# One level of a seven-product scheme in the value matmuls, with the weight sums streamed from DRAM

## The chip, the cores and the metric

The kernel runs on one core of a Trainium2 chip. Its engines work side by side: TensorE (PE; matmuls, with PEld for the weight loads), VectorE (DVE), ScalarE (ACT), GpSimd (POOL) and SyncE (SP), whose queue issues the DMAs here. The metric is the device time of one execution in microseconds.

## The reference

Local and global attention over 8 batches and 8 heads, and then a feed-forward on the attention's output, with a shift by one token:

```python
s_g = scale * q_g @ k_all^T;  out_g = softmax(s_g) @ v_all        # 32 global queries, all 544 keys
s_l = scale * [q_l @ k_g^T, q_l @ k_l^T within 32 positions]      # 512 local queries
out_l = softmax(s_l) @ [v_g, v_l]
x = concat([out_g, out_l])                      # (8, 544, 512): batch, tokens, heads x 64
x_prev = x shifted by one token, zero first
xk = mu_k * x + (1 - mu_k) * x_prev;  xr likewise with mu_r
k = relu(xk @ w_k)                              # 512 -> 1024
v = (k * k) @ w_v                               # 1024 -> 512
return sigmoid(xr @ w_r) * v
```

The weights w_k, w_v, w_r arrive as 64-bit floats.

## The kernel before

Everything is kept with features on the 128 partitions and tokens along the free side, 256 tokens (TOK) to a feed-forward step. A batch has two such halves of 256 local tokens; the 8 x 32 global tokens of all batches make one more set, done last. Heads are done in pairs of units, a unit being two heads.

A matmul operand of full precision is split into a high part (rounded to the PE's fp32r type by ACT) and a low part (the rest, a subtraction on POOL or DVE), and each product is made of three matmuls, high x high, high x low and low x high (`products`, L383 to L385). One such matmul has 128x128 weights and 256 columns. For one set of 256 tokens the keys take 8 x 4 x 3 = 96 of them, the gates 4 x 4 x 3 = 48, the values 4 x 8 x 3 = 96.

Weights come as chunks of 128x512 64-bit words (512 KB) into three buffers of the pool `stage`. `decode` (L171 to L182) makes 32-bit values of a chunk with one operation on ACT, three on DVE, and splits it with one on ACT and one on POOL. The high and low parts of all three weight matrices then stay in SBUF.

A pair of units runs through `scores` (matmuls L241, masked minimum on DVE L246, exponentials on ACT L251, normalizing on POOL L260), transposes on PE (L273, L282, L322) with copies out of PSUM, and `weighted` (L339, L352, L364). `weighted` begins with two banks of the PSUM tag "t", one of which the second reduction of `scores_global` (L303) reads until it is done. The result goes to `xT`. The feed-forward of a set is `mix` (L408 on DVE, L412 on DVE, L416 on ACT, L417 on POOL), `keys_and_gate` (keys: relu L429 on ACT, square L431 on POOL, high part L434 on ACT, low part L435 on DVE; gates: L446, or L449 and L451), and `values`, whose result is multiplied with the gate on DVE (L463) and stored by SP (L474, L479). All products of the feed-forward use two banks of PSUM, tag "m".

The order: the first batch's heads are done in halves while the weights of the keys arrive. Then `beside_heads` interleaves two generators in proportion to their numbers of steps: the heads of batch b, 32 steps, and the feed-forward of the batch before. The first such stage takes the heads of the second batch with the rest of the first batch's feed-forward (`rest_of_first`, 18 steps: two of keys, two of gates, six of keys and gates, eight of values, with a chunk or two decoded in each of the first ten). Later stages have 20 steps of 24 matmuls (the first of them 16): `feed_forward` makes the values of the set before while the mix of the next one is prepared. The last batch's feed-forward and the global tokens run alone. Within this program order a planner places each instruction by its own estimate of when its inputs are ready, and so also fixes the order in each engine's queue.

## Time and profile before

| | |
|---|---|
| median of 3 runs | 714.57 us (713.87 to 714.68) |
| the profiled execution | 713.56 us, span 711.8 us |
| PE, DVE, ACT, POOL busy | 684.2, 360.0, 394.8, 298.6 us |
| mean granted clock of PE | 0.978 |
| moved by DMA | 66.73 MB, mean 94 GB/s |

The profile shows one execution. "Busy" is the time that an engine has an instruction under way; matmuls overlap each other, so the spacing of their starts tells what one costs. L383 is line 383 of the kernel. "PE ps_t L339 <- DVE mg L303" in the waits says that PE's instruction of line 339, writing ps_t, waited for DVE's of line 303.

### The profile page before, as it was taken

Reading aid. Unit: us, or ns where it says so; the run is one execution under the profiler, and the core shown is the slowest. Engines: PE = TensorE matmul, PEld = TensorE weight load, DVE = VectorE, ACT = ScalarE, POOL = GpSimd, SP = SyncE. Lnnn points to the kernel's source line nnn. Section 1 sums busy time; section 2 is a strip of 40 time slices with the busy share of each in tenths; the row PEclk is TensorE's granted clock in tenths of the full one; section 3 lists DMA queues with packets and bytes.
Section 4 is the critical chain, followed back from the end, with each engine's and each line's share of the span. In section 5 each row is a group of like instructions: output and inputs, shape, how many; then the busy total and the mean of one; then the engine's idle time right before and its main releaser. Section 6 shows DMA issues by size and latency. Waiting matters only on the chain.

```text
span 711.8 us, 18514 instructions
## 1 busy us (share of the span) xinstructions
PE 684.2 (96%) x7616; PEld 645.3 (91%) x7616; DVE 360.0 (51%) x1134; ACT 394.8 (55%) x1075; POOL 298.6 (42%) x325
## 2 busy tenths in 40 slices
PE   5789799999999999999999999999999999999997
PEld 3568689989999999999999999899999999999997
DVE  5797976347254362736354363636354352534511
ACT  5877976365565565646565565646565553332420
POOL 6577685136253353424243353424243351323420
PEclk9788889999999999999999999999999999999999
DMA  8735334151423040403222040403222020000000
GB/s 343 279 98 205 128 124 167 39 179 38 158 74 107 16 164 31 164 32 96 98 84 97 17 163 31 164 30 107 88 90 91 16 80 26 17 16 30 2 30 30
DMA packets 21716, 66.73 MB, mean 94 GB/s; under 512 B 2176, under 2 KB 10880, under 8 KB 21632
## 3 DMA queue, kind: packets, MB, share of 16 engines
q1 hardware_dynamic: 21632, 65.55, 25.9%
q8 instruction: 60, 0.98, 0.6%
q14 instruction: 24, 0.20, 0.1%
HBM read 56.63 MB, written 8.91 MB: 92 GB/s over the span
## 4 chain that ended last, share of the span: by engine, by line
PE 77%; DVE 9%; ACT 7%; issue 3%; POOL 2%; DMA 2%; SPq 0%; POOLq 0%; DVEq 0%
PE ps_m L383 21%; PE ps_m L385 20%; PE ps_m L384 20%; PE ps_t L273 4%; PE ps_t L339 4%; PE ps_s L241 3%; ACT Pt L251 3%; DVE xfull L412 2%; PE ps_t L364 2%; DVE Pt L246 2%; POOL k L431 1%; DVE kkl L435 1%; DMA raw_qk<-qk 1%; PE ps_t L322 1%; PE ps_s L352 1%
## 5 line engine op out<-in xcount | busy, mean ns | idle before, releaser
L383 PE MATMUL ps_m<-xkh,wk_h 128*128 128x256 f32 x544 | 157.0, 290 | 2.5 <-ACT gate L446 2.5
L383 PE MATMUL ps_m<-kkh,wv_h 128*128 128x256 f32 x544 | 154.7, 284 | 0.0
L384 PE MATMUL ps_m<-xkl,wk_h 128*128 128x256 f32 x544 | 153.6, 283 | 0.0
L385 PE MATMUL ps_m<-xkh,wk_l 128*128 128x256 f32 x544 | 152.9, 281 | 0.0
L385 PE MATMUL ps_m<-kkh,wv_l 128*128 128x256 f32 x544 | 151.2, 278 | 0.3 <-POOL wv_l L182 0.3
L384 PE MATMUL ps_m<-kkl,wv_h 128*128 128x256 f32 x544 | 151.0, 278 | 0.0
L260 POOL TENSOR_TENSOR Pt<-Pt,ssum 128x512 f32<-128x512 f32 x64 | 67.8, 1060 | 156.0 <-DVE ssum L211 152.6
L251 ACT ACTIVATE Pt<-Pt,m 128x160 f32<-128x160 f32 x256 | 106.5, 417 | 40.6 <-DVE m L246 39.6
L431 POOL TENSOR_TENSOR k<-relu 128x512 f32<-128x512 f32 x68 | 73.4, 1079 | 125.8 <-ACT relu L429 125.8
L429 ACT ACTIVATE relu<-ps_m 128x512 f32<-128x512 f32 x68 | 40.6, 596 | 125.0 <-PE ps_m L385 122.8
L383 PEld LDWEIGHTS ps_m<-xkh,wk_h 128*128 128x128 f32 x544 | 104.0, 192 | 4.5 <-ACT gate L446 2.8
L383 PEld LDWEIGHTS ps_m<-kkh,wv_h 128*128 128x128 f32 x544 | 102.2, 188 | 3.6 <-issue 2.8
L384 PEld LDWEIGHTS ps_m<-xkl,wk_h 128*128 128x128 f32 x544 | 104.9, 193 | 0.0
L385 PEld LDWEIGHTS ps_m<-xkh,wk_l 128*128 128x128 f32 x544 | 104.0, 191 | 0.0
L385 PEld LDWEIGHTS ps_m<-kkh,wv_l 128*128 128x128 f32 x544 | 102.2, 188 | 0.5 <-POOL wv_l L182 0.5
L384 PEld LDWEIGHTS ps_m<-kkl,wv_h 128*128 128x128 f32 x544 | 102.2, 188 | 0.0
L435 DVE TENSOR_TENSOR kkl<-k,kkh 128x512 fp32r<-128x512 f32 x68 | 51.4, 756 | 98.0 <-POOL k L431 96.9
L246 DVE CUSTOM_DVE_ANT_0 Pt<-ps_s,masks 128x160 f32<-128x160 f32 x256 | 66.9, 318 | 45.7 <-PE ps_s L241 45.7
L383 PE MATMUL ps_m<-xrh,wr_h 128*128 128x256 f32 x272 | 79.6, 293 | 0.0
L384 PE MATMUL ps_m<-xrl,wr_h 128*128 128x256 f32 x272 | 76.9, 283 | 0.0
L385 PE MATMUL ps_m<-xrh,wr_l 128*128 128x256 f32 x272 | 76.8, 282 | 0.0
L417 POOL TENSOR_TENSOR xkl<-xfull,xkh 128x512 fp32r<-128x512 f32 x34 | 44.7, 1314 | 74.3 <-ACT xkh L416 74.3
(93 smaller groups left out, 1279.6 us busy)
## 6 DMA issues: line engine op xcount, KB each, us to landing
raw_qk<-qk SPq DMA_DIRECT2D x32, 768.0 KB, 5.7
raw_v<-v SPq DMA_DIRECT2D x32, 640.0 KB, 4.9
out_l<-gate SPq DMA_DIRECT2D x32, 256.0 KB, 2.2
w<-w_k SPq DMA_DIRECT2D x8, 512.0 KB, 9.3
w<-w_v SPq DMA_DIRECT2D x8, 512.0 KB, 3.6
w<-w_r SPq DMA_DIRECT2D x4, 512.0 KB, 3.9
out_g<-gate SPq DMA_DIRECT2D x2, 256.0 KB, 2.1
mu_k_sb<-mu_k SPq DMA_DIRECT2D x1, 2.0 KB, 11.2
```

What stands on the lines that cost most here:

```text
L246: nc.vector.tensor_tensor_reduce(out=Pt[:, i], in0=place(e, t, h), in1=masks[:, e, slots[t][1]], op0=ALU.add, op1=ALU.min, scale=-scale, s ...
L251: nc.scalar.activation(Pt[:, i], Pt[:, i], AF.Exp, bias=low_x[:, i:i + 1], scale=-1.0, accum_out=ssum[:, i:i + 1],)
L260: nc.gpsimd.tensor_mul(out, Pt[:, each, at:at + n], rinv.unsqueeze(2).to_broadcast([P, 4, n]))
L273: nc.tensor.transpose(tp[:, i], r.Pt[:, 4 * e + i, SG * e:SG * e + W], ident)
L339: nc.tensor.matmul(op[t][h * D:(h + 1) * D, j, e, a], s.v[:, h, i], r.PT[:, e, 2 * t + h, a * BL:(a + 1) * BL], start=(t, h) not in begun, ...
L383: nc.tensor.matmul(out, w_h[:, i, cols], x_h(i), start=(i == 0), stop=False)
L384: nc.tensor.matmul(out, w_h[:, i, cols], x_l(i), start=False, stop=False)
L385: nc.tensor.matmul(out, w_l[:, i, cols], x_h(i), start=False, stop=(i == n - 1))
L417: nc.gpsimd.tensor_sub(lo[:, both], xf, hi[:, both].bitcast(F32))
L429: nc.scalar.activation(rk, kp, AF.Relu)
L431: nc.gpsimd.tensor_mul(k2, rk, rk)
L435: nc.vector.tensor_sub(kl, k2, kh.bitcast(F32))
```

## The change

The values of a batch, 1024 -> 512 features for two halves of 256 tokens, are taken as a 2 x 2 product of blocks. The left side is the weights: A11, A12, A21, A22, each 256 output features by 512 input features. The right side is the squared keys: B11, B21 of the first half of tokens, B12, B22 of the second. Eight block products become seven, with four sums of weights S1 to S4 and four of keys T1 to T4 (Winograd's form of Strassen's scheme); a block product is 24 matmuls (`Keys.product`).

- The sums of weights are made once (`value_weights`, two chunks at a time). The high and low parts of all eight left blocks are written to a DRAM tile `scratch`, and w_v no longer stays in SBUF. Before each product its left block, 1 MB, is read back by two DMAs of SP (`load_left`) into five buffers of half a block each; the first two blocks are requested up front, and each product requests one more behind it. The global tokens' values stay four block products.
- The squared keys are kept unsplit (`k2p`, one buffer per block). The sums T1 to T4 are made by DVE on 128x1024 (`differences`), T1, T3 and T4 in the place of B11, B12 and B21. A block is split when it is near its use, by ACT and DVE (B) or by ACT and POOL (T).
- Products are joined in two banks "m" by going on accumulating in a bank, by copies to `sump` on ACT, and by additions on DVE. Two of a batch's four products with the gate are on POOL.
- Per batch `values_1` (three products) follows the first half's mix of the next batch, `values_2` (four products) that of the second half. So the first batch's values stand beside the third batch's heads instead of the second's: `rest_of_first` has ten steps, all of keys and gates, and the later stages 19. `mix` of the first batch's second half is called once for the keys and once for the gates.
- From the third batch on, each group of matmuls in `scores` and `weighted` is issued as one unbroken sequence (`Run`), whose first matmul waits for the copies and reductions that the group depends on.

```diff
-    gatep = ctx.enter_context(tc.tile_pool(name="gatep", bufs=2))
+    gatep = ctx.enter_context(tc.tile_pool(name="gatep", bufs=3))
     tmpp = ctx.enter_context(tc.tile_pool(name="tmpp", bufs=3))
-    mlp1 = ctx.enter_context(tc.tile_pool(name="mlp1", bufs=1))
-    mlp = ctx.enter_context(tc.tile_pool(name="mlp", bufs=2))
+    sump = ctx.enter_context(tc.tile_pool(name="sump", bufs=3))
+    k2p = ctx.enter_context(tc.tile_pool(name="k2p", bufs=1))
+    dramp = ctx.enter_context(tc.tile_pool(name="dramp", bufs=1, space=bass.MemoryType.DRAM))
     ps4 = ctx.enter_context(tc.tile_pool(name="ps4", bufs=4, space=PSUM))
...
+        order = list(range(src.shape[0] // P))
+        if src is w_v:
+            order = [i + a for i in range(NF // 2) for a in (0, NF // 2)]
...
+    LEFT = ("A11", "A21", "A12", "A22", "S1", "S2", "S3", "S4")
+    HC = NF // 2
...
+    def value_weights():
+        for i in range(HC):
+            A, S = (sums.tile([P, 4, 2, TOK], F32R, tag="x", name=f"left_{x}") for x in "as")
+            s = sums1.tile([P, 4, TOK], F32, tag="s", name="s")
+            a = []
+            for j in range(2):
+                val = decode(staged.pop(0), "s").rearrange("p (j n) -> p j n", j=2)
+                split(val, A[:, 2 * j:2 * j + 2, 0], A[:, 2 * j:2 * j + 2, 1])
+                a.append(val)
+            nc.vector.tensor_add(s[:, 0], a[0][:, 1], a[1][:, 1])
+            nc.vector.tensor_sub(s[:, 2], a[0][:, 0], a[0][:, 1])
+            nc.vector.tensor_sub(s[:, 1], s[:, 0], a[0][:, 0])
+            nc.vector.tensor_sub(s[:, 3], a[1][:, 0], s[:, 1])
+            split(s, S[:, :, 0], S[:, :, 1])
+            for j, part in ((0, A), (4, S)):
+                nc.sync.dma_start(out=scratch[:, j:j + 4, i], in_=part.bitcast(F32))
+            load_chunk()
+            load_chunk()
+            yield
+    V1 = (("A11", "B11"), ("A12", "B21"), ("S2", "T2"))
+    V2 = (("S3", "T3"), ("S1", "T1"), ("A22", "T4"), ("S4", "B22"))
+    to_load = [a for a, _ in V1 + V2] * B + ["A11", "A21", "A12", "A22"]
+    left = []
+    def load_left():
+        if to_load:
+            a = LEFT.index(to_load.pop(0))
+            for i in range(0, HC, 2):
+                part = leftp.tile([P, 2, 2, TOK], F32R, tag="a", name="a")
+                nc.sync.dma_start(out=part.bitcast(F32), in_=scratch[:, a, i:i + 2])
+                left.append(part)
...
+        run = Run(reads["s"] if slots[0][0].b > 1 else None)
...
+    class Run:
+        def __init__(self, copies=None):
+            self.copies, self.last = copies, None
+        def matmul(self, *a, **kw):
+            if self.copies is None:
+                nc.tensor.matmul(*a, **kw)
+                return
+            if self.last is not None:
+                with tc.issue_after(self.last.ins), tc.high_priority():
+                    self.last = nc.tensor.matmul(*a, **kw)
+                return
+            self.last = nc.tensor.matmul(*a, **kw)
+            for c in self.copies:
+                tc.add_manual_dep(
+                    self.last.ins, c.ins.name,
+                    mybir.DependencyInfo(mybir.DependencyClass.Sync, mybir.DependencyReason.DATA),
+                )
+    reads = {"s": []}
...
+    def weighted(units, xTs, PG=None, pairs=range(2), bank="s", copies=None):
...
-                nc.scalar.activation(kh, rk, AF.Square)
-                nc.vector.tensor_sub(kl, k2, kh.bitcast(F32))
...
+        def gates(self, whole_gate=True):
             self.gate = gatep.tile([P, NC, TOK], F32, tag="gate", name="gate")
...
                     nc.scalar.activation(self.gate, self.gate, AF.Sigmoid)
...
-            for e0 in range(0, NC, 2):
-                vp = psum("m").rearrange("p (j n) -> p j n", j=2)
+        def write(self, half, v):
+            es = slice(2 * half, 2 * half + 2)
+            o = self.gate[:, es]
...
+    class Keys:
+        def __init__(self, tokens):
+            self.tokens = tokens
+            self.k, self.parts = {}, {}
+        def block(self, name):
+            self.k[name] = k2p.tile([P, HC, TOK], F32, tag=name, name=name)
+            return self.k[name]
+        def keys(self, t):
+            n = self.tokens.index(t) + 1
+            return t.keys([self.block(f"B{i}{n}") for i in (1, 2)])
+        def differences(self):
+            k = self.k
+            k["T1"], k["T3"], k["T4"] = k["B11"], k["B12"], k["B21"]
+            for out, a, b in (("T1", "B12", "B11"), ("T2", "B22", "T1"), ("T3", "B22", "B12"), ("T4", "B21", "T2")):
+                nc.vector.tensor_sub(k[out] if out != "T2" else self.block("T2"), k[a], k[b])
+        def split(self, *names):
+            for b in names:
+                self.parts[b] = []
+                for i in range(0, HC, 2):
+                    h, l = (rightp.tile([P, 2, TOK], F32R, tag=x, name=f"b{x}") for x in "hl")
+                    split(self.k[b][:, i:i + 2], h, l, nc.vector if b[0] == "B" else nc.gpsimd)
+                    self.parts[b].append((h, l))
...
+        def product(self, out, b, fresh=True):
+            right = self.parts.pop(b)
+            for i in range(HC):
+                a, (b_h, b_l) = left[i // 2], right[i // 2]
                 for j in range(2):
...
+                    a_h, a_l = (a[:, i % 2, x, j * P:(j + 1) * P] for x in range(2))
+                    for n, (w, x) in enumerate(((a_h, b_h), (a_h, b_l), (a_l, b_h))):
+                        nc.tensor.matmul(
+                            out[:, j], w, x[:, i % 2], start=fresh and (i, j, n) == (0, 0, 0),
+                            stop=(i, n) == (HC - 1, 2), skip_group_check=True,
+                        )
+            del left[:HC // 2]
+            load_left()
...
+        def values_1(self):
+            t = self.tokens[0]
+            X, Y = self.bank(), self.bank()
+            self.product(X, "B11")
+            c11, self.u2 = self.sum(), self.sum()
+            nc.scalar.copy(c11, X)
+            yield
+            self.product(Y, "B21")
+            nc.vector.tensor_add(c11, Y, c11)
+            t.write(0, c11)
+            yield
+            self.product(X, "T2", fresh=False)
+            nc.scalar.copy(self.u2, X)
+            yield
+            self.split("T3", "T1", "T4")
+        def values_2(self):
+            t0, t1 = self.tokens
+            u2, u3 = self.u2, self.sum()
+            X, Y = self.bank(), self.bank()
+            self.product(X, "T3")
+            nc.vector.tensor_add(X, X, u2)
+            nc.scalar.copy(u3, X)
+            self.split("B22")
+            yield
+            self.product(Y, "T1")
+            nc.vector.tensor_add(u3, Y, u3)
+            t1.write(1, u3)
+            yield
+            self.product(X, "T4", fresh=False)
+            t0.write(1, X)
+            yield
+            self.product(Y, "B22", fresh=False)
+            nc.vector.tensor_add(u2, Y, u2)
+            t1.write(0, u2)
+            yield
+        def values_of_one(self):
+            t, = self.tokens
+            banks = self.bank(), self.bank()
+            for b in range(2):
+                parts = self.parts[f"B{b + 1}1"]
+                for e, out in enumerate(banks):
+                    self.parts[f"B{b + 1}1"] = parts
+                    self.product(out, f"B{b + 1}1", fresh=not b)
+                    if b:
+                        t.write(e, out)
+                    yield
...
+    FF_STEPS = 6
+    V_STEPS = len(V1) + len(V2)
...
-    def feed_forward(tokens, before):
-        for t in tokens:
+    def feed_forward(this, before):
+        for n, t in enumerate(this.tokens):
             t.mix()
-            if before is not None:
-                yield from before.values()
-            yield from t.keys_and_gate()
-            before = t
+            yield from (before.values_1, before.values_2)[n]()
+            if n:
+                this.split("B11", "B21")
+            yield from this.keys(t)
+            if n:
+                this.differences()
+                this.split("T2")
+            yield from t.gates()
     PAIR_STEPS = 8
...
+                weighted(pair, xTs, PG, copies=A.copies + C.copies + [copy, reads["g"]] if pair[0].b > 1 else None)
             for s in nxt or ():
...
-            yield
-        for t in first:
-            yield from t.values()
+        yield from first[0].gates(whole_gate=False)
+        first[1].mix("r")
+        yield from first[1].gates(whole_gate=False)
...
+        leftp, rightp = place(ctx, "leftp", 5, side="right"), place(ctx, "rightp", 6, side="right")
+        load_left()
+        load_left()
+        last.split("B11", "B21")
+        last.differences()
+        last.split("T2")
+    leftp = rightp = None
     beside_heads(rest_of_first(), 2 * FF_STEPS - 2)
-    last = None
+    before = last
     for b in range(1, B):
-        tokens = tokens_of(b) + ([global_tokens()] if b == B - 1 else [])
-        steps = feed_forward(tokens, last), FF_STEPS * len(tokens) - (4 if last is None else 0)
+        this = Keys(tokens_of(b))
+        steps = feed_forward(this, before), 2 * FF_STEPS + V_STEPS
         if b < B - 1:
             beside_heads(*steps)
-        last = tokens[-1]
-    for _ in steps[0]:
-        pass
-    for _ in last.values():
+        before = this
+    final = Keys([global_tokens()])
+    t, = final.tokens
...
+        yield from steps[0]
+        t.mix()
+        yield from before.values_1()
+        yield from final.keys(t)
+        yield from t.gates()
+        yield from before.values_2()
+        final.split("B11", "B21")
+        yield from final.values_of_one()
+    for _ in end():
         pass
```

116 lines of the change are left out of this document (58 added, 58 removed).

## The prediction

> **What bounds the kernel now.** I read the head of the page first (busy shares, 40 slices, chain), then the busy time by stretch, then the waits.
>
> ```profile
> span 711.8 us, 18514 instructions
> PE 684.2 (96%) x7616; PEld 645.3 (91%) x7616; DVE 360.0 (51%) x1134; ACT 394.8 (55%) x1075; POOL 298.6 (42%) x325
> ...
> PE   5789799999999999999999999999999999999997
> ...
> ACT  5877976365565565646565565646565553332420
> ...
> PEclk9788889999999999999999999999999999999999
> ```
>
> From the seventh slice on TensorE never rests and the others are half idle; in the first six DVE and ACT are as full as PE, and PE's clock is not always whole. So there are two regimes. The stretches (columns: busy us and count of PE, PEld, DVE, ACT, POOL; granted clock; DMA share; GB/s) put numbers to them:
>
> ```profile
> core 0: us, PE busy (x) PEld busy (x) DVE busy (x) ACT busy (x) POOL busy (x), PEclk, DMA share, GB/s
> 62.00:115.00 53.00, 48.27 (x518) 43.12 (x517) 44.71 (x119) 45.49 (x116) 35.76 (x33) 0.90 0.45 146
> 115.00:149.00 34.00, 33.68 (x407) 31.97 (x408) 14.04 (x57) 14.18 (x50) 12.43 (x15) 1.00 0.29 107
> 208.80:248.70 39.90, 39.51 (x462) 37.77 (x462) 19.07 (x67) 23.25 (x64) 15.52 (x17) 1.00 0.25 87
> 614.46:625.34 10.88, 10.88 (x98) 10.88 (x97) 3.28 (x4) 2.31 (x3) 3.67 (x3) 1.00 0.07 26
> 636.22:641.98 5.76, 5.76 (x50) 5.76 (x49) 4.50 (x8) 1.85 (x3) 2.45 (x2) 1.00 0.00 0
> ```
>
> 62 to 149 us is the stage in which the second batch's heads run beside the first batch's feed-forward. Until 115 us DVE and ACT are 84% and 86% busy, with queues that wait for each other: that is their limit. From 115 us on PE alone is full. The third row is one steady period, a pair of heads and half a feed-forward. The last two rows are runs of 96 value matmuls and of 48 gate matmuls (the counts take in a neighbour at each edge): 10.88/96 = 113.3 ns and 5.76/48 = 120.0 ns apiece.
>
> **The change, part by part.**
>
> *Products.* A batch's values take 2 x 96 = 192 matmuls now and 7 x 24 = 168 after, of the same shape; the global tokens keep 96. Over eight batches 192 fewer: 192 x 113.3 ns = 21.8 us of PE. If the new operands run at the gates' 120.0 ns instead, the 1344 that stay cost 1344 x 6.7 ns = 9.0 us more; I take 0, since shape and order of an (h, l) triple are the same, and keep 9.0 for the range.
>
> *Where the saving lands.* After 149 us the old kernel has 14 x 240 + 240 = 3600 feed-forward matmuls left. The new one, once its first stage is over, has 8 x 168 values, 14 x 144 keys and gates and 240 of the global tokens: 3600 as well. Heads are equal. So the whole gain is what the first stage gets shorter: it loses all of the first batch's 192 value matmuls. PE needs 48.27 + 33.68 - 21.8 = 60.2 us there; the old stage was 87 us, 65.2 without its values. But those values were PE work that filled the time after DVE and ACT had finished. Their new load, from these groups (out<-in, shape, count | busy us, mean ns | idle before, releaser):
>
> ```profile
> L435 DVE TENSOR_TENSOR kkl<-k,kkh 128x512 fp32r<-128x512 f32 x68 | 51.4, 756 | 98.0 <-POOL k L431 96.9 <-PE ps_m L384 1.1
> L434 ACT ACTIVATE kkh<-relu 128x512 fp32r<-128x512 f32 x68 | 43.3, 636 | 1.6
> L463 DVE TENSOR_TENSOR gate<-ps_m,gate 128x512 f32<-128x512 f32 x34 | 23.5, 691 | 94.1 <-PE ps_m L385 94.1
> L408 DVE TENSOR_TENSOR diff<-xT 128x256 f32<-128x256 f32 x64 | 32.3, 543 | 14.8 <-ACT xT L375 14.3
> L412 DVE SCALAR_TENSOR_TENSOR xfull<-diff,mu_r_sb,xT 128x256 f32<-128x256 f32 x64 | 46.6, 763 | 13.8 <-POOL xkl L417 13.8
> L412 DVE SCALAR_TENSOR_TENSOR xfull<-diff,mu_k_sb,xT 128x256 f32<-128x256 f32 x64 | 36.0, 598 | 1.2 <-POOL xkl L417 1.2
> L417 POOL TENSOR_TENSOR xkl<-xfull,xkh 128x512 fp32r<-128x512 f32 x34 | 44.7, 1314 | 74.3 <-ACT xkh L416 74.3
> L416 ACT CAST xkh<-xfull 128x512 fp32r<-128x512 f32 x34 | 20.9, 616 | 29.2 <-DVE xfull L412 29.2
> L181 ACT CAST wv_h<-w 128x512 fp32r<-128x512 f32 x8 | 5.3, 662 | 0.6 <-DVE w L178 0.6
> ...
> 117.34 1.48 POOL L182 TENSOR_TENSOR wv_l<-w,wv_h 128x512 fp32r<-128x512 f32 x1
> ```
>
> DVE, 62 to 149 us: 44.71 + 14.04 = 58.8. Off: 6 kkl (4.5), 4 gate products (2.8), and the second batch's mix, which now stands beside values (4 x 0.543 + 8 x 0.68 = 7.6; 0.68 is the mean of L412's two rows). On: 16 sums and differences of 128x256 in the weight combinations (8.7 at L408's price), 4 differences more since the second half's mix is made in two goes (2.2), 4 differences of 128x1024 of the squared keys (8 x 0.756 = 6.0), 4 splits of B11 and B21 (3.0). Result 63.8. ACT: 59.7 - 6 x 0.636 - 4 x 0.616 of the moved mix + 8 x 0.66 for casting S (its 128x1024 is no cast of this trace; the bounds are one and two casts of 128x512, and I take two) + 6 x 0.616 = 62.4. POOL: 48.2 + 8 x 1.31 (S) + 2 x 1.31 (T2) - 4 x 1.31 = 56.1. All three pass or near PE's 60.2, and DVE at its 84% needs 63.8/0.844 = 75.6 us. The stage ends at 62 + 75.6 = 137.6 instead of 149: **-11.4 us**; 10.4 of the 21.8 are lost as PE idle time. Bounds: -21.8 (PE stays the limit) and 0.
>
> The route of the left blocks lies inside this stage: weight sums to DRAM (8.4 MB), then two blocks back, only after the early pools close, so after the last split. The last row is the last weight chunk's split, at 117 us; with the sums about 10 us later, and the values are not first needed before 137. Hidden; without that cover it costs the landing shown below.
>
> *Heads' matmuls in one run.* Today a pair's last products start before all banks are free:
>
> ```profile
> 492.33 0.49 PE L352 MATMUL ps_s<-PG,raw_v 128*64 128x32 f32 x10
> 493.22 0.69 PE L339 MATMUL ps_t<-PT,raw_v 128*64 128x64 f32 x16 [0.40 <-DVE mg L303]
> ...
> PE ps_t L339 <- DVE mg L303: 3.9, 10, 0.4
> ```
>
> The new dependencies put this wait ahead of the first matmul, where a feed-forward block can be issued instead. Queued behind that first matmul are only the rest of its run; those who wait for them are ACT's copies to xT, with a mix as cover. **-3.9 us**; bounds -5 and +3.9 (the wait stays and covers the whole run).
>
> *Steady batches.* By twice the third row, per batch: ACT 46.5 - 8 x 0.636 + 14 x 0.616 + 3 PSUM copies (1.8) = 51.8; DVE 38.1 + 5.8 (6.0 for the differences, 4.5 for six splits, 4.1 for six products and sums out of PSUM at L463's price, less 6.0 for kkl and 2.8 for gate products); POOL 31.0 + 8 x 1.31 + 2 gate products (2.2) = 43.7; in a period of 79.8 - 2.7 = 77.1 us. No new bound. New waits: three products (T2, T4, B22) go on in a bank that ACT or DVE has just read or written, each with one 24-matmul product (2.7 us) as cover against a copy of 0.6. Bounds: 0, and 24 such places at the 0.40 us that is the one wait left in a steady pair, 9.6. I take **+3**: the old schedule, with alike chains of relu, square and split, shows one surviving wait per pair.
>
> *End without heads.* Blocks are fetched as two loads of 512 KB, 2.5 blocks ahead:
>
> ```profile
> q1 hardware_dynamic: 21632, 65.55, 25.9%
> ...
> raw_qk<-qk SPq DMA_DIRECT2D x32, 768.0 KB, 5.7
> ...
> w<-w_v SPq DMA_DIRECT2D x8, 512.0 KB, 3.6
> ```
>
> The last eight products stand back to back: 2.72 us each for 1.05 MB. The queue moved 65.55 MB in 25.9% of 711.8 us, 355 GB/s while busy, or 2.95 us a block; eight times 0.23 us are covered by the lead. At the rate of two raw_qk loads together (1.57 MB in 5.7 us, 3.8 us a block) 5.5 blocks fall 6 us behind, and the lead takes back 3.2. I take **+1.5**, bounds 0 and 6.
>
> **Sum**, against the profiled execution's 713.6 us (span 711.8): 713.6 - 11.4 - 3.9 + 3 + 1.5 = 702.8. Its time lies 1.0 us under the median shown, 714.6; on the median's scale 703.8, and I say 703.5. A measurement of this kernel tells about 0.2%, 1.4 us, from no change.
>
> **The rivals.**
>
> *The start stays as long as it was.* PE, with less to do, idles and loses its clock; that happens already:
>
> ```profile
> 80.00:85.00 5.00, 2.53 (x24) 1.82 (x24) 4.79 (x15) 4.94 (x10) 5.00 (x7) 1.00 0.00 0
> 85.00:90.00 5.00, 2.79 (x17) 2.07 (x14) 4.94 (x15) 4.97 (x16) 3.79 (x3) 0.51 0.53 153
> 90.00:95.00 5.00, 5.00 (x25) 5.00 (x24) 3.24 (x7) 3.93 (x13) 4.33 (x5) 0.50 0.16 60
> ...
> 55.30 0.41 PE L383 MATMUL ps_m<-xkh,wk_h 128*128 128x256 f32 x1
> 55.52 0.41 PE L384 MATMUL ps_m<-xkl,wk_h 128*128 128x256 f32 x1
> ...
> 83.40 0.39 PE L383 MATMUL ps_m<-xkh,wk_h 128*128 128x256 f32 x1 [2.47 <-ACT gate L446]
> ...
> 89.67 0.69 PE L282 MATMUL ps_t<-ident,Pgl 128*128 128x128 f32 x2 [2.21 <-ACT PT L275]
> ...
> L435 DVE TENSOR_TENSOR kkl<-k,kkh x68: 682/693/1823, 62.2 to 693.3; 128x512 fp32r<-128x512 f32 x68
> ...
> 98.66 1.82 DVE L435 TENSOR_TENSOR kkl<-k,kkh 128x512 fp32r<-128x512 f32 x1
> ...
> 98.61 1.32 POOL L182 TENSOR_TENSOR wv_l<-w,wv_h 128x512 fp32r<-128x512 f32 x1 [1.64 <-ACT wv_h L181]
> ```
>
> At half clock matmuls start 0.21 us apart, not 0.113. If the stage's 240 keys and gates all ran so, PE would need 60.2 + 24 = 84 us, and the stage would end near 147: 713.6 - 2 - 3.9 + 4.5 + 1 = 713. The Trainium skill, "TensorE: Matmul & The Clock Gate", section "Why this matters for your kernels", says the same danger: a gap of some 3 us between bursts halves the clock. By that rule the idle time that I forecast would be paid twice, and this rival's time would be the result; here the two gaps of 2.47 and 2.21 us go with a cold stretch of ten. A second way to the same time is the collision of DVE and POOL: the L435 row gives its shortest, median and longest in ns, and the longest, 1.82 us against 0.69, ran while POOL made a split (last two rows). For it: more two-input work on both engines, in this very stage. Against: from 80 to 85 us PE was half idle and its clock stayed whole.
>
> *PE keeps the whole saving.* If DVE's work overlaps better, the stage is PE's and ends at 127: 704 - 10.4 = 693. For it: POOL and ACT have gaps until 115. Against: DVE's sum.
>
> *Slower: blocks arrive late.* SP's queue is in order, and it stands at stores:
>
> ```profile
> SPq L474 <- DVE gate L463: 210.5, 21, 28.2
> ```
>
> A block's load queued behind a store whose product is still running is issued only at its end, and then the 3.6 us landing meets a 2.7 us product. Four stores a batch, 32 in all, each delaying PE by 3.6 - 2.7 = 0.9 us, give +29; if half of them do, 704 + 15 = 719. It decides from 0.33 us a store on (10.6/32). Against: two blocks are always ahead, and heads lie between most products.
>
> **How the numbers follow.** Forecast 0.68; start as long as before 0.10 (half of it within 0.2%, the rest split); whole saving 0.09; late blocks 0.13. The forecast's own range, from its bounds: 696 to 711. The range of 692 to 714 takes in the whole saving and the long start and leaves out the late blocks and some of the spread at 120 ns: about 0.17. Faster 0.68 + 0.09 + 0.03 = 0.80; same 0.05; slower 0.15.
>
> **What would show it.** Right: PE under 90% busy somewhere from 100 to 137 us while DVE is full; the first values of the batch near 137; steady periods of 77 us a batch; no wait of L339's kind on DVE mg; block loads never among PE's releasers before the last 25 us. Wrong: PE waits for DMA blocks, value matmuls at 120 ns, steady periods of 79 us or more, or a first stage that ends at 127 or after 147.

## The result, and the profile after

The changed kernel takes 749.34 us median (748.53 to 757.44) against 714.22 of the kernel before on the same chip: ratio 1.0517, 95% interval 1.0445 to 1.059. The forecast was 703.5 with a range of 692 to 714; the change makes the kernel slower by 35 us. The profiled execution took 748.53 us. The head of its page, with PE's and the clock's slices:

```profile
span 746.7 us, 18633 instructions
...
PE 682.7 (91%) x7424; PEld 639.9 (86%) x7424; DVE 428.3 (57%) x1178; ACT 428.3 (57%) x1151; POOL 427.6 (57%) x417
...
PE   5889777679998999899999999899989999898997
...
PEclk9779898899999999999999999999999999999899
```

192 matmuls fewer, and PE is as long busy as before (684.2), because some of what is left runs on a halved clock and at a wider spacing. PE is no longer full: 91% instead of 96%, and digits under 9 return in almost every batch.

I cut both spans into stages where ACT writes the last copy of a batch's heads to `xT`: the second batch's stage, the third's, the fourth to seventh, the eighth, and the end without heads. First the kernel before, then the changed one (columns as in the prediction):

```profile
66.40:151.20 84.80, 79.75 (x899) 73.09 (x898) 55.21 (x171) 57.94 (x163) 44.43 (x44) 0.94 0.39 130
151.20:218.00 66.80, 66.41 (x804) 61.86 (x804) 33.99 (x130) 40.99 (x125) 31.18 (x33) 1.00 0.27 97
218.00:537.60 319.60, 316.45 (x3691) 302.54 (x3690) 153.83 (x529) 185.87 (x513) 126.26 (x136) 1.00 0.25 87
537.60:612.80 75.20, 74.81 (x849) 72.75 (x848) 33.10 (x92) 36.34 (x88) 25.43 (x25) 1.00 0.14 49
612.80:711.80 99.00, 95.27 (x832) 95.07 (x830) 33.58 (x55) 25.87 (x39) 26.88 (x23) 1.00 0.07 22
```
```profile
64.90:150.90 86.00, 64.41 (x720) 55.51 (x723) 69.21 (x186) 62.59 (x168) 53.45 (x46) 0.88 0.60 210
150.90:241.40 90.50, 83.80 (x922) 79.46 (x914) 53.43 (x144) 50.31 (x140) 55.21 (x51) 0.96 0.55 196
241.40:561.90 320.50, 308.90 (x3594) 294.71 (x3593) 175.35 (x542) 198.50 (x550) 184.94 (x180) 0.99 0.51 179
561.90:628.70 66.80, 66.80 (x779) 64.84 (x778) 35.85 (x88) 36.18 (x94) 37.24 (x34) 1.00 0.43 157
628.70:746.70 118.00, 107.70 (x879) 106.34 (x878) 49.77 (x70) 35.61 (x59) 54.16 (x43) 0.97 0.47 161
```

Against what fewer matmuls alone would give at 113.3 ns, with the matmuls counted as the rows above count them (PE's x):

| part | before | after | matmuls more or fewer | above that |
|---|---|---|---|---|
| end of the second batch's heads | 151.2 | 150.9 | none counted on: what is saved here (179 in the stage) is idle time | -0.3 |
| third batch's stage | 66.8 | 90.5 | +118 = +13.4 | +10.3 |
| four steady stages | 319.6 | 320.5 | -97 = -11.0 | +11.9 |
| last stage and end | 174.2 | 184.8 | -23 = -2.6 | +13.2 |

By the program's steps the third batch's stage has only 72 matmuls more, and the last part has 24 more; in the trace PE had made some 47 of the later ones by the time the third batch's heads ended, so the table goes by the trace's counts. The last column adds up to 35.1 us; the spans differ by 34.9. So four questions: why the first stage is as long as it was though PE has 15 us less to do in it, and what the third batch's stage, the steady stages and the end lost. The waits of the changed kernel name the steady loss:

```profile
PE ps_m L575 <- DVE gate L527: 17.6, 6, 3.1
PE ps_s L328 <- DMA raw_qk<-qk: 8.2, 5, 5.3
PE ps_m L575 <- ACT sum L593: 5.3, 2, 3.3
PE ps_s L328 <- DVE w L184: 4.8, 2, 3.4
```

Once a batch the first matmul of a value product (L575) waits 3 us for DVE's copy of the gates out of PSUM (L527), which frees the bank; four of the six waits, 11.6 us, lie in the steady stages. DVE's timeline around the first of them, in the third batch's stage, and then PE in the wait and behind it (by stretch):

```profile
222.35 2.12 DVE L558 TENSOR_TENSOR T<-B,B 128x1024 f32<-128x1024 f32 x1
224.39 1.21 DVE L558 TENSOR_TENSOR B<-B,B 128x1024 f32<-128x1024 f32 x1
225.53 2.98 DVE L496 SCALAR_TENSOR_TENSOR xfull<-diff,mu_r_sb,xT 128x256 f32<-128x256 f32 x2
228.43 0.31 DVE L301 CUSTOM_DVE_ANT_0 Pt<-ps_s,masks 128x160 f32<-128x160 f32 x1
...
229.68 1.22 DVE L558 TENSOR_TENSOR B<-B,T 128x1024 f32<-128x1024 f32 x1
...
230.91 0.65 DVE L527 COPY gate<-ps_m 128x512 f32<-128x512 f32 x1
```
```profile
228.00:231.50 3.50, 0.71 (x6) 0.51 (x5) 3.50 (x15) 2.56 (x10) 0.66 (x2) 0.99 0.27 111
231.50:236.00 4.50, 4.38 (x26) 4.25 (x28) 1.43 (x6) 3.84 (x6) 3.70 (x6) 0.63 0.13 12
```

The gates are done at 228.7, but their copy stands behind differences of the squared keys (L558), a mix and the heads' reductions in DVE's queue. Behind the gap PE's clock is 0.63 for 4.5 us; after four of the six such waits (230, 310, 470 and 689 us) it falls, after those at 390 and 550 it does not. The Trainium skill, "TensorE: Matmul & The Clock Gate", section "What's actually happening", has the clock halve after an idle window of about 3.4 us on a free-running window. The trace agrees with a free-running window, since alike gaps cost the clock in some cases and not in others; it doesn't agree with the length, since these gaps were of 2.9 to 3.1 us.

### The profile page after: what moved, and what is told of

Its sections match the earlier page's. It is cut to its first block, busy times and chain, and to the rows that moved or that the text cites. A ratio compares the mean times of both kernels' runs of the same rounds, so it can differ in the third digit from the quotient of the medians.

```text
span 746.7 us, 18633 instructions
## 1 busy us (share of the span) xinstructions
PE 682.7 (91%) x7424; PEld 639.9 (86%) x7424; DVE 428.3 (57%) x1178; ACT 428.3 (57%) x1151; POOL 427.6 (57%) x417
## 3 DMA queue, kind: packets, MB, share of 16 engines
q1 hardware_dynamic: 43136, 136.86, 51.8%
## 4 chain that ended last, share of the span: by engine, by line
PE 68%; DVE 16%; ACT 7%; issue 3%; DMA 2%; POOL 2%; SPq 0%; POOLq 0%; ACTq 0%; DVEq 0%
PE ps_m L575 22%; PE ps_m L464 10%; PE ps_m L465 10%; PE ps_m L466 10%; PE ps_t L332 5%; DVE xfull L496 4%; PE ps_s L332 4%; ACT Pt L307 3%; PE ps_t L353 3%; DVE B L558 2%; DVE Pt L301 2%; DVE T L558 2%; PE ps_s L334 1%; PE ps_t L378 1%; DVE diff L492 1%
## 5 line engine op out<-in xcount | busy, mean ns | idle before, releaser
L575 PE MATMUL ps_m<-bh,a 128*128 128x256 f32 x960 | 192.1, 294 | 24.6 <-DVE gate L527 17.6
L575 PEld LDWEIGHTS ps_m<-bh,a 128*128 128x128 f32 x960 | 158.7, 198 | 28.2 <-DVE gate L527 18.8
L575 PE MATMUL ps_m<-bl,a 128*128 128x256 f32 x480 | 140.0, 292 | 0.0
L316 POOL TENSOR_TENSOR Pt<-Pt,ssum 128x512 f32<-128x512 f32 x64 | 69.8, 1091 | 84.8 <-DVE ssum L265 81.6
L512 POOL TENSOR_TENSOR B<-relu 128x512 f32<-128x512 f32 x68 | 72.6, 1070 | 69.8 <-ACT relu L511 69.8
L575 PEld LDWEIGHTS ps_m<-bl,a 128*128 128x128 f32 x480 | 95.2, 198 | 0.6
L191 POOL TENSOR_TENSOR bl<-B,bh 128x512 fp32r<-128x512 f32 x48 | 63.0, 1335 | 24.5 <-ACT bh L190 24.5
L496 DVE SCALAR_TENSOR_TENSOR xfull<-diff,mu_r_sb,xT 128x256 f32<-128x256 f32 x64 | 61.7, 991 | 15.4 <-POOL B L512 12.6
L190 ACT CAST bh<-B 128x512 fp32r<-128x512 f32 x100 | 60.9, 623 | 16.4 <-PE ps_m L575 15.1
```

Of the source, the lines that this page charges most:

```text
L190: nc.scalar.copy(hi, val)
L191: (engine or nc.gpsimd).tensor_sub(lo, val, hi.bitcast(F32))
L316: nc.gpsimd.tensor_mul(out, Pt[:, each, at:at + n], rinv.unsqueeze(2).to_broadcast([P, 4, n]))
L496: nc.vector.scalar_tensor_tensor(self.shape(xf[:, j]), self.shape(diff[:, j]), mu[:, c0 + j:c0 + j + 1], self.prev(c0 + j), op0=ALU.mult, ...
L512: nc.gpsimd.tensor_mul(k2[f0 // HC][:, f0 % HC:f0 % HC + 2], rk, rk)
L575: nc.tensor.matmul(out[:, j], w, x[:, i % 2], start=fresh and (i, j, n) == (0, 0, 0), stop=(i, n) == (HC - 1, 2), skip_group_check=True,)
```

## The experiments

I worked with these theories. A: in the steady stages DVE's queue makes PE wait. B: the value matmuls are spaced by where their operands lie. C: the vector work of preparing the value weights holds the first two stages. D: what is lost is DVE's stretching of operations while POOL works, so relieving POOL helps. E: the order of the feed-forward around the values matters. Ratios are to the kernel before, with their 95% intervals; 1% is 7.1 us.

**The steady wait (A and D).**

*e1_order*: the differences and T2's split follow the gates in the program.

```diff
             yield from this.keys(t)
-            if n:
-                this.differences()
-                this.split("T2")
             yield from t.gates()
+            if n:
+                this.differences()
+                this.split("T2")
```

> The differences and T2's split stand behind the gates instead of ahead of them; nothing else. Theory A (in each steady batch TensorE waits some 3.1 us for the gate copies of line 527, because DVE makes the 128x1024 differences first; six such waits, 17.6 us): the six waits go, and the time falls by 12 to 18 us, to 731 to 737. Rival (the waits only move: T2 is then late and TensorE waits ahead of the third product): the time stays within 3 us, and T2's split (line 190 or 191) is named as the releaser instead.

1.052 (1.0503 to 1.0537). The wait is the same (17.9 us, 7 times): the planner, which orders by its own estimate of readiness, put DVE's instructions in the same order as before. Program order tests nothing here.

*e2_gact*: the gates' copies out of PSUM (L527) are made by ACT.

```diff
-                nc.vector.tensor_copy(self.gate[:, e0:e0 + 2], rp)
+                nc.scalar.copy(self.gate[:, e0:e0 + 2], rp)
```

> The gates' two copies out of PSUM are made by ACT instead of DVE; the differences stay where they are. Theory A: DVE's queue no longer stands between the gates and the values, the six waits of 3.1 us go, and the time falls by 10 to 18 us (ACT has 0.6 us a copy more). Rival (ACT, with its exponentials, is as late as DVE was): the same waits with ACT named, time within 3 us.

1.0295 (1.0274 to 1.0316): 16 us less. Waits, and the four steady stages:

```profile
PE ps_m L575 <- ACT gate L527: 6.4, 6, 1.1
```
```profile
241.40:551.80 310.40, 305.93 (x3593) 291.89 (x3593) 164.91 (x524) 206.98 (x565) 182.72 (x180) 1.00 0.51 184
```

The wait is a third of what it was, the clock whole, a period 77.6 us instead of 80.1; these four stages give 10.1 of the 16 us. Theory A holds, with a smaller wait left, now for ACT.

*e7_sqact*: ACT makes the keys' squares instead of POOL (L512).

```diff
-                nc.gpsimd.tensor_mul(k2[f0 // HC][:, f0 % HC:f0 % HC + 2], rk, rk)
+                nc.scalar.activation(k2[f0 // HC][:, f0 % HC:f0 % HC + 2], rk, AF.Square)
```

> The changed kernel, with the 68 squares of the keys made by ACT (0.64 us each) instead of POOL (1.07 us each); DVE's instructions are the same ones. Theory D (DVE's operations with two SBUF inputs last up to three times as long while POOL works, and this makes DVE late): DVE's busy time falls from 428 by 8 us or more although it has the same work, TensorE's waits for DVE gate shrink, and the time falls by 8 us or more. Rival (DVE is late because it has more instructions): DVE's time stays, the waits stay, and ACT's 43 us more make the time the same or longer.

1.0553 (1.0534 to 1.0572), no gain. POOL's busy time fell from 427.6 to 363.5 us, DVE's only from 428.3 to 424.4. Theory D falls as a remedy, though the stretching is there: in the changed kernel, shortest, median and longest in ns,

```profile
L558 DVE TENSOR_TENSOR T<-B,B x8: 1196/2120/2297, 151.5 to 682.7; 128x1024 f32<-128x1024 f32 x8
L558 DVE TENSOR_TENSOR B<-B,B x16: 1209/1218/2054, 149.6 to 684.9; 128x1024 f32<-128x1024 f32 x16
L492 DVE TENSOR_TENSOR diff<-xT x68: 407/419/1510, 30.5 to 656.9; 128x256 f32<-128x256 f32 x68
```

and in e7 other operations are the long ones:

```profile
L558 DVE TENSOR_TENSOR T<-B,B x8: 1190/1225/1226, 150.7 to 687.1; 128x1024 f32<-128x1024 f32 x8
L558 DVE TENSOR_TENSOR B<-B,B x16: 1224/2062/2325, 147.5 to 688.2; 128x1024 f32<-128x1024 f32 x16
```

**The spacing (B).** In the compiled programs (no view of the profile shows addresses) the value weights and their moving operands begin at byte addresses with the same remainder modulo 128, 96 and 96, in the changed kernel, and so do the gates', 32 and 32, in both kernels; the operands of the products that ran at 113 ns begin at 96 and 32. *e3_padv* puts 64 bytes between the pools of the two operands of the values; *e11_b_padg* puts as much before the gate weights in the kernel before.

```diff
-        leftp, rightp = place(ctx, "leftp", 5, side="right"), place(ctx, "rightp", 6, side="right")
+        leftp = place(ctx, "leftp", 5, side="right")
+        place(ctx, "shift", side="right").tile([P, 16], F32, tag="shift", name="shift")
+        rightp = place(ctx, "rightp", 6, side="right")
```

```diff
+    shiftp = ctx.enter_context(tc.tile_pool(name="shiftp", bufs=1, reuse_waits="tile"))      # e11
+    shiftp.tile([P, 16], F32, name="shift")
     gatew = ctx.enter_context(tc.tile_pool(name="gatew", bufs=1, reuse_waits="tile"))
```

> The pool of split keys is moved by 64 bytes, so that the values' weights and moving operand no longer have the same address modulo 128. Theory B (matmuls of 128x256 start 120 ns apart where the two addresses agree modulo 128, and 113 where they don't: before, keys and values 96 against 32 and 113 ns, gates 32 against 32 and 120 ns; after, values 96 against 96 and 120 ns): values at 113 ns, 1440 x 6.6 ns = 9 us less, to 740. Rival (the spacing comes from busier engines and DMAs): values stay at 120 ns, time the same.

> The kernel before with the gate weights moved by 64 bytes, nothing else. Theory B: the gates' 816 matmuls at 113 instead of 120 ns, up to 5.4 us less, 707 to 709. Rival (what TensorE saves turns into waits for the heads, as the 1.7 us of the version with sequences suggests): 711 to 712.

e3 gave 1.046 (1.0427 to 1.0494). The same 4 us of value products, in the changed kernel and in e3 (the counts take in two or three matmuls that began before):

```profile
658.50:662.50 4.00, 4.00 (x36) 4.00 (x35) 2.63 (x4) 3.27 (x6) 2.55 (x2) 1.00 0.46 132
```
```profile
658.50:662.50 4.00, 4.00 (x38) 4.00 (x37) 2.63 (x4) 3.27 (x6) 2.56 (x2) 1.00 0.54 154
```

The median distance of starts is 120 ns in the first and 113 in the second; e11's gates went from 120 to 113 too. So B holds for the spacing, as far as two shifts of 64 bytes show it. Its price in time is smaller than the sum says: e3 gained 4 us of 9 (clear of noise against e1, whose engines run in the changed kernel's order, though not against that kernel's own wider interval), with the DVE wait unchanged (17.4 us in 6) and the long runs of keys, whose addresses did not change, at 118 ns instead of 113 (96 in 11.31 us), which nothing here explains. e11 gained nothing, 0.9996 (0.9986 to 1.0007): PE was busy 679.3 us instead of 684.2 and idle that much longer.

**Unbroken groups.** *e5_b_run* gives the kernel before the class `Run`, as in the change, and *e6_b_run_padg* adds e11's 64 bytes. *e12_norun* takes it out of the changed kernel, *e10_run3* lets it begin at the fourth batch.

```diff
-            self.copies, self.last = copies, None      # e12
+            self.copies, self.last = None, None
-        run = Run(reads["s"] if slots[0][0].b > 1 else None)      # e10, likewise in weighted
+        run = Run(reads["s"] if slots[0][0].b > 2 else None)
```

> The kernel before, with the unbroken sequences of scores and weighted (Run) and nothing else of the change. The prediction's step: the wait of line 339 on DVE mg goes (3.9 us in ten places), time 708 to 711. Rival (the wait stays, ahead of the sequence, or the planner's order gets worse): 713 or more.

> The same, and the gate weights moved by 64 bytes, so that they lie 96 modulo 128 against 32 for their moving operand. Theory B: the 816 gate matmuls at 113 instead of 120 ns, 5.4 us less than with Run alone, 703 to 706. Rival (the address plays no part in the gates): as with Run alone.

> The changed kernel without the unbroken sequences. If they gain in the steady batches what they gained in the old kernel (1.7 us in all) and cost 4 us in the start: time 2 to 3 us less, 746. If they hold off TensorE in the new kernel's fuller queues: 5 us less or more. If they are worth the predicted 3.9 us: 753.

> The changed kernel with the unbroken sequences from the fourth batch on instead of the third, nothing else. Theory E: in the start TensorE no longer stands at the first matmul of the third batch's scores (line 334, 4.2 us at 132 us); time 4 to 6 us less, 743 to 745. Rival (DVE and ACT would hold it at the next matmul anyway): within 2 us.

e5: 0.9981 (0.9972 to 0.9991); e6: 0.995 (0.9938 to 0.9963), 709.5 us, short of the 703 to 706 expected but the fastest version that computes the whole reference; e10: 1.0558 (1.0508 to 1.0607); e12: 1.0814 (1.0758 to 1.0869), which every theory missed. In the old kernel the ten waits of 0.4 us went, and five of 0.7 came at PE's next transposes; 1.4 us of the 3.9 were gained. e10 moves nothing: in the changed kernel one batch more or less of it shows no difference. In the changed kernel the same class is worth 21 us (1.0814 against 1.0517). e12's waits and, around one of them, its stretches:

```profile
PE ps_t L328 <- DVE mg L379: 8.8, 5, 1.8
```
```profile
475.00:480.00 5.00, 3.24 (x52) 2.93 (x49) 5.00 (x16) 2.05 (x9) 2.10 (x2) 0.92 0.25 104
480.00:485.00 5.00, 5.00 (x45) 4.44 (x45) 2.73 (x11) 2.32 (x6) 3.60 (x6) 0.50 0.02 3
485.00:490.00 5.00, 5.00 (x26) 4.78 (x25) 1.57 (x3) 1.42 (x4) 1.07 (x2) 0.55 0.68 236
```

It is the same DVE queue: T, B and the mix stand before the reduction mg, PE's group starts and stops in front of it, and then runs ten us at half clock (40 matmuls of heads in 3.9 us, gates 214 ns apart). In the changed kernel the group is held until its inputs are there, and gates are issued in that time. Whether the small matmuls or the gap alone cost the clock was not tried.

**The first two stages (C).** *e4_nos* leaves the sums S1 to S4 out of the changed kernel (not added, split or stored; A blocks are read in their place). *e13_nowv* leaves out the whole preparation of the value weights and stores the raw chunks instead, so that loads, stores and block reads stay.

```diff
-            nc.vector.tensor_add(s[:, 0], a[0][:, 1], a[1][:, 1])      # e4, and the three sums behind it
-            split(s, S[:, :, 0], S[:, :, 1])
-            for j, part in ((0, A), (4, S)):
+            for j, part in ((0, A),):
...
-            a = LEFT.index(to_load.pop(0))
+            a = LEFT.index(to_load.pop(0)) % 4
```
```diff
-                val = decode(staged.pop(0), "s").rearrange("p (j n) -> p j n", j=2)      # e13
...
-            split(s, S[:, :, 0], S[:, :, 1])
-            for j, part in ((0, A), (4, S)):
-                nc.sync.dma_start(out=scratch[:, j:j + 4, i], in_=part.bitcast(F32))
+                w64 = staged.pop(0).bitcast(F32).rearrange("p (j s n) -> p j s n", j=2, s=2)
+                for k in (2 * j, 4 + 2 * j):
+                    nc.sync.dma_start(out=scratch[:, k:k + 2, i], in_=w64)
```

> The sums S1 to S4 of the weights are not made, split or written (the four products that use them read A blocks instead, so this leaves out part of the computation); everything else stays, with the same loads and products. Theory C (the start is held by the vector engines' work for the weights, of which this is 7 us of DVE, 4 of ACT, 10 of POOL and half of the writes): the first values start by 135 instead of 152 us and the time falls by 10 to 20 us. Rival (the start is held by the heads' and keys' own chains, once the first batch's values no longer fill TensorE): it falls by less than 5 us.

> The changed kernel with the value weights not prepared on chip: each loaded chunk goes straight to the scratch tile, so the loads, the 8.4 MB of stores and the reads of left blocks stay, and the decoding, the splits and the sums S1 to S4 (ACT, DVE, POOL) are left out; the left blocks hold raw words. If the engines' queues, filled by this preparation, hold the first two stages (theory C): 152 us instead of 151 for the end of the second batch's heads becomes 128 to 138, the third batch's 241 becomes 205 to 220, and the time falls to 715 to 728 from 749. If the DMAs (stores and reads) or the chain of heads hold them (rival): both ends move by less than 5 us, and the time stays above 740.

e4: 1.0331 (1.0289 to 1.0374), 13 us less. e13: 1.026 (1.0206 to 1.0314), 18 us less. The second batch's heads end at 146.7 and 141.1 us instead of 150.9, the third's at 227.7 and 222.0 instead of 241.4. The first values start at 133 and 130 us instead of 152. e4 came as expected; e13 moved the same way, but by a little less than expected in all three figures. The DMA traffic, which e13 keeps, isn't what holds them. C holds.

*e8_best1* joins e2 and e3, which had helped, with e11's 64 bytes and with three moves that were not tried alone: one sigmoid per half in the first batch (`whole_gate`), a fourth stage buffer and a fourth early chunk.

```diff
-    stage = place(early_s, "stage", 3, side="right")
+    stage = place(early_s, "stage", 4, side="right")
...
-    for _ in range(3):
+    for _ in range(4):
         load_chunk()
...
-        yield from first[0].gates(whole_gate=False)      # likewise first[1]
+        yield from first[0].gates()
```

> The changed kernel with gate copies on ACT, split keys and gate weights moved by 64 bytes, one sigmoid for each half of the first batch too, and four buffers for weight chunks instead of three. By theories A and B: 734 of the gate copies alone, less 9 for the values and 5 for the gates at 113 ns, 720; if buffers and ACT's table loads hold the start, up to 10 less, 710. Rival (the start is held by the amount of vector work and what TensorE saves is lost in waits): 725 to 730, with the first values not before 150 us.

1.0064 (1.0043 to 1.0086), 717.33 us: 31 of the 35 us are back, and the four steady stages take 308.2 us, 77.05 each. What remains is the start. There PE stood still for 5.75 us before a group's first matmul; DVE's and PE's rows:

```profile
120.39 1.51 DVE L220 TENSOR_TENSOR s<-w,w 128x256 f32<-128x256 f32 x1 [0.36 <-POOL left_s L191]
121.82 1.25 DVE L221 TENSOR_TENSOR s<-w 128x256 f32<-128x256 f32 x1
123.00 0.61 DVE L222 TENSOR_TENSOR s<-s,w 128x256 f32<-128x256 f32 x1
123.65 1.37 DVE L223 TENSOR_TENSOR s<-w,s 128x256 f32<-128x256 f32 x1
124.94 0.31 DVE L301 CUSTOM_DVE_ANT_0 Pt<-ps_s,masks 128x160 f32<-128x160 f32 x1
...
127.07 0.50 PE L334 MATMUL ps_s<-raw_qk 64*64 64x160 f32 x1 [5.75 <-issue]
```

The page calls it "issue", but the matmul starts just after the last of eight reductions (126.9), which began only when the four sums were done: 4.7 us of DVE at the stretched rate, where 4 x 0.41 would be 1.6. *e14_best1_nowv* is e8 with e13's edit, *e18_best1_nos* e8 with e4's. *e15_best1_run3* is e8 with e10's edit; *e16_best1_spool* moves the four sums to POOL.

```diff
-            nc.vector.tensor_add(s[:, 0], a[0][:, 1], a[1][:, 1])      # e16, likewise the other three
+            nc.gpsimd.tensor_add(s[:, 0], a[0][:, 1], a[1][:, 1])
```

> The best version of the new scheme so far (717) with the same part left out. Theory C: the third batch's heads end at 195 to 208 instead of 226, and the time is 690 to 700, under the old kernel's 714: seven products would win if their weights came prepared. Rival: more than 708, so even free preparation would bring less than 1 per cent.

> The best version of the new scheme (717) with only the sums S1 to S4 left out (not added, not split, not stored; the A blocks are read in their place), decoding and splits of A kept. Leaving out the whole preparation brought 19 us, and leaving out the sums in the changed kernel 13. If the sums are the larger part: 702 to 707. If decoding and splits, which the old kernel has too, are the larger part: 709 to 715.

> The best version of the new scheme so far (717) with unbroken groups from the fourth batch on instead of the third. In its trace the first matmul of such a group in the start waits 5.7 us (121.3 to 127.1 us), and it starts 0.07 us after the last of DVE's eight reductions. If that wait is what holds the third batch's heads: 711 to 714. If the reductions are late for any kind of issue, because DVE makes the weight sums first (theory C): 716 to 719, the same wait now at another line.

> The best version of the new scheme so far (717) with the four weight sums S1 to S4 of each of four steps made by POOL instead of DVE. If it is DVE's queue alone that holds the heads in the start (the sums take 4.7 us of it in each step): 711 to 714. If the whole chain of preparation counts, whichever engine it stands on, or POOL then stands in the way of its own normalizing and splits: 716 to 725.

e14: 0.981 (0.9794 to 0.9826), 698.61 us; e18: 0.990 (0.9872 to 0.9927); e15: 1.0155 (1.0135 to 1.0176); e16: 1.0092 (1.0075 to 1.0109). e8's first two stages, then e14's:

```profile
66.30:146.40 80.10, 60.49 (x705) 52.68 (x704) 65.28 (x176) 57.95 (x156) 54.61 (x47) 0.89 0.68 241
146.40:226.00 79.60, 78.23 (x895) 74.93 (x894) 46.02 (x135) 50.91 (x142) 49.05 (x47) 0.99 0.54 196
```
```profile
65.90:131.90 66.00, 56.66 (x703) 50.24 (x702) 42.30 (x138) 46.70 (x140) 36.22 (x37) 0.97 0.80 298
131.90:208.10 76.20, 74.83 (x898) 71.35 (x897) 41.52 (x134) 50.25 (x142) 45.74 (x45) 1.00 0.53 193
```

The same matmuls, and without the preparation the first stage is 14 us shorter. Two thirds of the 2.5% are the sums (e18: 1.6%), which only the new kernel has. e15 went past both expectations: unbroken groups at the third batch are worth 6 us in this version. e16 shows that the chain counts, not DVE alone: moved to POOL, the sums let the first stage end 3 us sooner (143.3), but the next takes 7 us longer and ends 4 us later (229.6), with a wait of 4.5 us for a block from DRAM.

*e9_best2*: e8 with `Run` from the fourth batch, the mix behind the first product, and the gates between the last product groups (E).

```diff
-            t.mix()
-            yield from (before.values_1, before.values_2)[n]()
+            values = (before.values_1, before.values_2)[n]()
+            next(values)
+            t.mix()
+            yield
+            yield from values
...
-        yield from t.gates()
         yield from before.values_2()
+        yield from t.gates()
```

> As the version with 717 us, and three more moves: the unbroken sequences only from the fourth batch on, the next mix behind the first block product instead of ahead of it, and in the end the global gates between the last two groups of four products. Theory E (the rest of the loss is waits that a place in a queue makes: 4 to 9 us of the sequences' first matmul in the start, 5 us of ACT's copies behind the mix in the end, 3 us of block loads): 700 to 707, faster than the kernel before. Rival (the vector engines' amount of work in the start sets it): 712 to 716.

1.0121 (1.0107 to 1.0135), worse than e8 and outside both expectations. e15 has the first of the three moves alone and is slower still, so that move is the loss. The other two together gain some 0.3%, with intervals of e9 and e15 that touch, so E is not shown; neither was measured alone.

*e17_b_best_nowv*: e6 with its eight value chunks copied raw to SBUF, the counterpart of e14.

```diff
         hi, lo = high[:, i, cs], low[:, i, cs]
+        if n >= NK + NC:
+            for k, part in enumerate((hi, lo)):
+                nc.sync.dma_start(out=part.bitcast(F32), in_=w64.bitcast(F32)[:, k * CH:(k + 1) * CH])
+            return
```

> The fastest eight-product version (709.5: the old kernel with unbroken groups and the gate weights moved by 64 bytes) with its value weights not prepared either: each of the eight last chunks is copied raw into the high and low parts by DMA, and decoding and splits are left out. It is the counterpart of e14 (698.6), so that the seven products are compared without the preparation on both sides. If the seven products are worth their PE time once the preparation is gone: 702 to 708, above e14. If the old kernel gains as much from it as the new one (18 us): 692 to 699, not above e14, and the scheme has nothing to give.

0.9838 (0.9819 to 0.9857), 702.27 us. It gains 1.1% from it, e8 gained 2.5%. With no preparation on either side the seven products are 0.3% ahead, with intervals that just overlap: not shown to be faster. With decoding and splits on both sides, and the sums neither made nor stored, they are: e18 0.990 (0.9872 to 0.9927) against e6 0.995 (0.9938 to 0.9963). The sums then cost 1.6%.

## Why the prediction was wrong, by its steps

The sum gave 702.8 us for the profiled execution, which took 748.5. Of the difference, 11.1 us are in the first stage, 10.3 in the third batch's, 8.9 in the steady stages, 11.7 in the last stage and end, and 3.9 are the term of the unbroken groups, whose real effect is inside the measured stages.

**The first stage, -11.4 us: measured -0.3.** This is the step that failed first: the stage's length. It took DVE's work and divided by the 84% that DVE had been busy. The work was nearly right:

```profile
62.00:149.00 87.00, 66.07 (x731) 56.89 (x731) 67.31 (x183) 62.00 (x165) 54.61 (x48) 0.88 0.59 205
```

DVE 67.3 against 63.8, ACT 62.0 against 62.4, POOL 54.6 against 56.1. The sums were priced at L408's mean of 0.543 us and took 0.95 on average. But the stage isn't limited by a sum of busy times. Each step of the preparation goes DMA, ACT, DVE, ACT, POOL and back into DVE's queue, and the heads' reductions stand in the same queue; PE starves behind them, at clock 0.88. DVE was 77% busy, not 84%. 137.6 had been forecast for its end; in e8, which has other remedies too, it ended at 146.4, without the sums at 140.2 (e18) and without the preparation at 131.9 (e14). The first values came at 152 us.

The rival "the start stays as long as it was" had the mechanism (collision, idle PE, lost clock) and its time, 713, for that stage alone. It stopped there; the stage after it lost 10.3 us more, of which no term of mine held anything. Its waits and cold stretches account for that, by my estimate: some 5 us around 160 us (3.3 us for a sum's copy on ACT, then values 213 ns apart for 3.4 us), 4.6 at its end (the wait of 2.9 us for the gates' copy, with as long a cold stretch behind it), and about 1 for the spacing.

**Steady batches, +3 in all: measured +11.9 in four batches.** Engine sums were near (per batch DVE 43.8 us against 43.9, ACT 49.6 against 51.8, POOL 46.2 against 43.7), and "no new bound" was right. The period of 77.1 us was met in e8 with 77.05, which is in part luck, since e8 has its gates at 113 ns and still waits for copies on ACT. Wrong was to look for new waits only at the three products that reuse a bank, at the 0.40 us of a surviving wait. The wait came where an old copy (L527) stood on an engine that had been given four operations of 128x1024 a batch: 2.9 us, not 0.4. Everything on the list of what would show me wrong came true: steady periods of 79 us or more (80.1), value matmuls at 120 ns, a first stage that ends after 147 (150.9), and waits for blocks, though only 1.5 us of them.

**Spacing, taken as 0 because shape and order are the same: it was 120 ns,** my upper bound, 9.0 us by the count. The reason for choosing 0 was no reason; two spacings for one shape stood in the rows that I quoted.

**Unbroken groups, -3.9: -1.4 by e5** in the old kernel: the waits of 0.4 us went, and others of 0.7 came at PE's next transposes. In the new kernel it is worth 21 us against a state that I never priced.

**End without heads, +1.5:** the last stage and the end came out 13.2 too long. By my estimate half of that is a wait of 3.1 us for DVE's gate copy with 6.8 us of half clock behind it (3.4 us lost), 3.8 are the spacing of 570 value matmuls, 2.0 a wait for ACT's sum, and 0.9 the blocks. The late blocks, the one rival on the slower side, did not occur: PE waited 1.5 us for them in two places. So the sign that I gave 0.15 came by a way that was none of the rivals.

## What to carry to other kernels

Work that is taken off the bounding engine and paid on the others has to be put into their queues, in order: write down, for each engine, what stands in front of the instruction that frees the bounding engine's next bank, and price that, not the busy share. A copy that frees a bank belongs on the engine with the shorter queue in front of it at that moment (here 16 us for one line). And a saving in a stage that is bound by a chain is not a saving: first see whether the stage is full.

## What the runs showed that I had not expected

- Where weights and moving operand began at the same remainder modulo 128 bytes (96 and 96, 32 and 32), matmuls of 128x128 by 256 started 120 ns apart, and at 96 and 32 mostly 113 (e3, e11: a shift of 64 bytes changes it). The keys of e3, at 96 and 32 too, ran at 118 ns and don't fit this.
- DVE operations with two inputs in SBUF took up to 3.7 times as long (differences of 128x256, from 0.41 to 1.51 us) and 1.9 times (128x1024, from 1.20 to 2.30) where POOL worked beside them. The Trainium skill, "GPSIMD Engine Reference", section "1. Specifications", names this contention without a size. Taking 64 us of work from POOL did not lessen it (e7).
- Small gaps before small matmuls (1.8 us, e12) were followed by ten us of half clock, while gaps of 2.9 to 3.1 us in front of value products cost the clock in four cases of six.
